# States' tokens in rounds of 64 + 32 + 32 rows, a new order of the small steps, and another order of the first loads

## The chip, the core and the metric

The kernel runs on one core of one Trainium2 chip. The metric is the device time of one execution in microseconds (us). Every run of the kernel before is listed with its median; one more execution was profiled, and all times of single instructions come from that one.

## The reference, cut to what matters

`x` has 8 batches of 8 heads x 512 tokens x 64, `state` 8 batches of 8 heads x 32 x 64. Attention goes both ways, and its two results are joined along the token axis, so a batch has 512 tokens read from the states (below: text tokens) and 32 read from the text (below: states' tokens). A switch layer with 8 experts follows; all is float32.

```python
xread = softmax(x @ state.T * 0.125) @ state        # 512 rows a batch
sread = softmax(state @ x.T * 0.125) @ x            #  32 rows a batch
t = concat([xread, sread])  ->  4352 rows of 512    # heads side by side
e = argmax(t @ w_gate); g = softmax(t @ w_gate)[e]
out = g * (relu(t @ w1[e]) @ w2[e])                 # w1: 512 x 1024, w2: 1024 x 512
```

On the given inputs all 512 text tokens of a batch choose one expert: 1, 2, 7, 0, 0, 0, 3 and 4 for batches 0 to 7. The states' tokens are handled in two halves of 128 rows (batches 0 to 3 and 4 to 7). Counted with the reference, the experts 0 to 7 get 0, 56, 0, 29, 1, 40, 0 and 2 rows of the first half, and 32, 64, 0, 0, 0, 0, 0 and 32 of the second.

## The kernel before, in words

Every engine runs its instructions in the order in which the program writes them; waits are semaphores. TensorE is PE in the profile, VectorE DVE, ScalarE ACT, GpSimd POOL, SyncE SP. A float32 product of 128 x 512 is two PE instructions, so counts of matmuls in the profile are twice those of the calls.

**Start** (L118 to L169, L715 to L736). SP loads the states of batch 0, `x` of batch 0, the other states and `x` of batch 1. Then it reads the guessed expert of batch 0 (`guess`, L201) and loads that expert's w1 (2 MB, `load_w1`, L237) and w2 (2 MB, `load_w2`, L421). Pool meanwhile clears DRAM: 12 DMAs for the two `g_dram` buffers (L162) and 6 for the two `ss_dram` buffers (L166).

**Batch 0** (`in_full`, L427) is computed in full: `G = state @ w1` (`states_w1`, L399), 8 products `ph` with a relu, and 4 x 8 products `py`.

**Batches 1 to 7** (`batch`, L546) use that a relu over a batch's tokens is often all on or all off. `lists(b)` (L458) makes G, transposes it (`pgt`), sorts the hidden units with a count (`rank`, L497) and scatters their rows into `g_dram` by 8 indirect DMAs from Pool (L509). `fetch(b)` (L515) loads the sorted rows back (`gp`, 3 DMAs) and gathers rows of w2 by 6 indirect DMAs from Pool (`gather`, L524, tile `w2c`). `mask(b)` (L534) zeroes unused rows on DVE. `batch(b)` then makes `pgu` (4 transposes), `pm` (2 x 4 products with `w2c`), `phu` (2 x 2 products) and `py`.

**Attention** of a batch is `front` (L285: transposes and softmax on DVE and ACT, products `pa`) and `back` (L308: transposes of `a2`, products `pw`, `pl`, routing, `pq`, `pcnt`; it loads `x` two batches ahead).

**The states' tokens** (`sort_states`, L591; `rounds`, L641). A half's 128 rows are scattered into `ss_dram` by expert in groups of 32 rows, each group of one expert. A round takes 4 groups: it loads its 128 rows (`xg`), transposes them (`ptx`), and multiplies by w1 (tile `pgh`, two halves) and, after another transpose (`pth`), by w2 (tile `pgy`, two halves). Each half is 4 parts; a part is one slot of a ring of weights (`s`), of 4 tiles of 256 KB, one per group, loaded by SP under a condition that skips groups without rows. `four` (L665) runs a part's 4 products of 32 columns each. The ring has 4 slots, and `fetch(4)` refills it after each half. The first half of the states' tokens has 2 rounds, the second 1; more rounds run only if `more` is above 0 at the end.

**The order by hand.** `inserts` (L813) takes a string for each place between PE's large products; each letter there runs one step of a generator: A attention (`back(b)` and `front(b+1)` a step each), S `lists`, F `fetching`, M `masking`, R the states' tokens, K constants. Batches 1 to 7 share one string of 13 places (L831). Place 1 is behind `pgu`, 2 to 4 inside `pm`, 5 and 6 behind the two `phu`, 7 to 12 between the `py`; in it the scatters of the next batch (last step of `lists`) stand at place 3, the loads of `fetch` and the first three gathers at 6, the mask and the other gathers at 8.

Of the kernel before, what the change touches and what calls it, by code (L numbers as in the profile page):

```python
# [20 lines left out]
def kernel(  # L21
# [57 lines left out]
    NT = 2  # L79
    NG = 12  # L80
    NR = NG // 4
    MAIN = (2, 1)
    RING = 4

# [6 lines left out]
    st_dram = dram.tile([B * NS, DM], FP32)  # L91
    ss_dram = [dram.tile([NG * 32, XW], I32, name=f"ss_dram{t}") for t in range(NT)]
    g_dram = [dram.tile([CAPP + CAPU, GW], FP32, name=f"g_dram{i}") for i in range(2)]
# [29 lines left out]
    load_states(2, B - 1, B)  # L123
    load_x(1, sp)

# [19 lines left out]
    rev8 = iota("rev8", [128, E], [[-1, E]], base=E)  # L145
    jio = iota("jio", [128, NG], [[1, NG]])
    pos8 = iota("pos8", [128, NFC], [[128, NFC]], step=1)
# [10 lines left out]
    gp.memset(blank[:], 0)  # L158
    for i in range(2):
        for r in range(0, CAPP + CAPU, 128):  # L160
            n = min(128, CAPP + CAPU - r)
            gp.dma_start(out=g_dram[i][ds(r, n)].bitcast(I32), in_=blank[0:n, 0:GW])  # L162
    gp.memset(blank[:, DM + 1:DM + 2], FAR)
    for t in range(NT):
        for r in range(NR):
            gp.dma_start(out=ss_dram[t][ts(r, 128)], in_=blank[:])  # L166

# [243 lines left out]

    rings = [sst.tile([128, 4, 512], FP32, name=f"s{i}") for i in range(RING)]

# [7 lines left out]
    def load_w2(e):  # L421
        w2x = [ring() for _ in range(2)]
        for u in range(2):
            sp.dma_start(out=w2x[u][:], in_=moe_w2[ds(e, 1), ts(u, 512)].rearrange("o (c p) f -> p (o c) f", p=128))
        return w2x

    def in_full(G, a, w2x, store, insert=None):  # L427
        hx = [ring() for _ in range(2)]
        for f in range(NFC):
            ph = bank(name="ph")  # L430
            for g in range(2):
                pe.matmul(ph[:], lhsT=G[g][:, ts(f, 128)], rhs=tokens_of(a)[:, g], start=(g == 0), stop=(g == 1))
            relu(hx[f // 4][:, f % 4], ph[:])
            if insert:
                insert()
        for c in range(NC):
            py = bank(name="py")
            for f in range(NFC):
                pe.matmul(py[:], lhsT=hx[f // 4][:, f % 4, ts(c, 128)], rhs=w2x[f // 4][:, f % 4, :],
                          start=(f == 0), stop=(f == NFC - 1))  # L440
                if insert and f == 3:
                    insert()
            store(c, py)
            if insert:
                insert()
# [69 lines left out]
    def fetch(b):  # L515

        t = gps[b] = ffn.tile([128, NP + NU, GW], FP32, tag="gp", bufs=2, name="gp")
        gp.dma_start(out=t[:, 0:NP + 1], in_=g_dram[b % 2][0:CAPP + 128].rearrange("(j p) k -> p j k", p=128))
        for u in range(2):
            gp.dma_start(out=t[ts(u, 64), NP + 1], in_=g_dram[b % 2][ds(CAPP + 128, 64)])  # L520
        w2cs[b] = []
        gather(b, 3)

# [64 lines left out]

    eg = [const.tile([128, NR, 2, 4], I32, name=f"eg{t}") for t in range(NT)]

    def sort_states(t):  # L591
# [11 lines left out]
        for c in range(NDC):  # L603
# [8 lines left out]
        pe.matmul(pr[:, 1, :], lhsT=ones_b[:], rhs=oh[:, NX + t, :], start=True, stop=True, skip_group_check=True)  # L612
        small = lambda n, w=E, dt=FP32: att.tile([128, w], dt, tag=n, name=n)
        ng_i, ng, cum, base, rk = small("t_ni", dt=I32), small("t_ng"), small("t_cum"), small("t_base"), small("t_rk")
        dve.tensor_scalar(ng_i[:], pr[:, 1, :], 31.0, None, ALU.add)
        dve.tensor_scalar(ng_i[:], ng_i[:], 5, None, ALU.logical_shift_right)
        dve.tensor_copy(out=ng[:], in_=ng_i[:])
        dve.tensor_tensor_scan(cum[:], ng[:], none[:, 0:E], 0.0, ALU.add, ALU.add)
        dve.tensor_tensor(base[:], cum[:], ng[:], ALU.subtract)
        dve.scalar_tensor_tensor(rk[:], base[:], 32.0, pr[:, 0, :], ALU.mult, ALU.add)  # L620
        dve.tensor_tensor(rk[:], rk[:], oh[:, NX + t, :], ALU.mult)
        slot, slot_i = small("t_sl", 1), small("t_si", 1, I32)
        dve.tensor_reduce(slot[:], rk[:], AX.X, ALU.add)
        dve.tensor_copy(out=slot_i[:], in_=slot[:])
# [3 lines left out]
            out=ss_dram[t][:], out_offset=bass.IndirectOffsetOnAxis(ap=slot_i[:, 0:1], axis=0),  # L628
            in_=srow[:].bitcast(I32), in_offset=None, bounds_check=NG * 32 - 1, oob_is_err=False)
        ge = att.tile([128, NG, E], FP32, tag="t_ge", name="t_ge")  # L630
        dve.tensor_tensor(ge[:], jio[:].unsqueeze(2).to_broadcast([128, NG, E]),
                          cum[:].unsqueeze(1).to_broadcast([128, NG, E]), ALU.is_ge)
        eg_f = small("t_eg", NG)
        dve.tensor_reduce(eg_f[:], ge[:], AX.X, ALU.add)
        dve.tensor_scalar(eg_f[:], eg_f[:], float(E - 1), None, ALU.min)
        dve.tensor_copy(out=eg[t][:, :, 0], in_=eg_f[:].rearrange("p (r q) -> p r q", q=4))
        dve.tensor_scalar(eg[t][:, :, 1], jio[:].rearrange("p (r q) -> p r q", q=4), cum[:, E - 1:E], None, ALU.is_lt)
        dve.tensor_scalar(more[:, t:t + 1], cum[:, E - 1:E], -4.0 * MAIN[t], 0.0, ALU.add, ALU.max)
        yield

    def rounds(t, r0, r1):  # L641
# [9 lines left out]
        def fetch(n):  # L651
            for _ in range(n):
                if parts:
                    r, kind, k, half = parts.pop(0)
                    if r not in ex:
                        round_in(r)
                    w = ring()
                    for q in range(4):
                        src = (moe_w1[ds(ex[r][q], 1), ts(k, 128), ts(half, 512)] if kind == 1
                               else moe_w2[ds(ex[r][q], 1), ts(k, 128), :])  # L660
                        sp.dma_start(out=w[:, q], in_=src.rearrange("o p f -> p (o f)"),
                                     cond=ex[r][4 + q], bounds_check="skip_entire_dma")
                    have[r, kind, k, half] = w

        def four(dst, lhsT, r, kind, k, half, start, stop):  # L665
            w = have.pop((r, kind, k, half))
            for q in range(4):
                pe.matmul(dst[ts(q, 32), :], lhsT=lhsT[:, ts(q, 32)], rhs=w[:, q, :], start=start, stop=stop,
                          skip_group_check=True)

        round_in(r0)
        fetch(RING)
        for _ in range(2):
            yield
        for r in range(r0, r1):
# [46 lines left out]
    load_w1(0, expert_of(eb, 0))  # L722
    w2x = load_w2(expert_of(eb, 0))
    for t in std[1:]:
        act.copy(t[:, :, 64:128], t[:, :, 0:64])
        act.copy(t[:, :, 128:160], t[:, :, 0:32])
    next(f0)
    next(f0)
# [34 lines left out]

    attended, done, summed, listed, fetched = [0], [0], [0], [0], [0]

    def attention():
        for b in range(B):
            while done[0] < b - 3:
                yield
            for _ in run(back(b), *([front(b + 1)] if b + 1 < B else [])):  # L770
                yield
            attended[0] = b + 1
            yield

# [9 lines left out]
    def fetching():  # L784
        for b in range(1, B):
            while listed[0] < b or done[0] < b - 1:
                yield
            fetch(b)
            fetched[0] = b
            yield  # L790
            while summed[0] < b - 1:
                yield
            gather(b, NP + NU - 3)
            yield

    def masking():
        for b in range(1, B):
            while b not in w2cs or len(w2cs[b]) < NP + NU:
                for k in "SF":
                    next(todo[k], None)  # L800
# [9 lines left out]

    todo = {"A": attention(), "S": listing(), "F": fetching(), "M": masking(), "R": tokens(), "K": late_constants()}

    def inserts(plan):  # L813
        steps = iter(plan.split(","))

# [4 lines left out]

    next(todo["A"])
    G = [sst.tile([128, F], FP32, tag=n, name="G0") for n in ("sh", "shT")]
# [4 lines left out]
    load_next_w1(1)  # L827
    in_full(G, aTs[0], w2x, store_batch(0), inserts("A,A,AK,AAS,AAS,AS,AAS,AS,AAS,SAA,SAA,FAA,FSAA,SAA,SA,SAM"))
    for b in range(1, B):
        done[0] = b  # L830
        batch(b, inserts("FS,SA,SR,SA,SR,FS,SA,MSR,A,R,A,AR,R"))  # L831
    for k in "ASFMR":
        for _ in todo[k]:
            pass
# [27 lines left out]

    with tc.If(number(rest_i[0:1, 0:1], B * E + NT * NG) > 0):
        with tc.If(number(n_i[0:1, 1:2], NT * NG) > 0):
            for t in range(NT):
# [102 lines left out]
```

## Time and profile before

| what | us |
|---|---|
| median of 9 runs (lowest, highest) | 469.44 (464.05, 476.36) |
| the profiled execution | 467.46 |
| its span, first to last instruction | 465.6 |
| PE busy | 395.1 (85%) |
| DVE busy | 197.9 (42%) |
| ACT busy | 123.8 (27%) |
| Pool busy | 133.2 (29%) |
| mean granted clock of TensorE | 0.949 of full speed |
| moved by DMA | 105.54 MB, 46.9% of the engines' time on SP's queue, 16.7% on Pool's |
| first `pgu` of batches 1 to 7 | 117.2, 156.0, 220.7, 287.9, 327.8, 377.6, 436.0 |
| last product's end | 459.6 |

Busy times are those of each engine alone and lie beside one another. A matmul's end is modelled, so PE's busy time holds some waiting; where PE is seen to wait, the releaser in brackets behind a row tells for what. A chain row "DMA s" means that the step after it could not start before that transfer of the states' weights had landed.

### The profile page before, as it was taken

To read this page: it belongs to the slowest core of one execution; us is meant where nothing else is said; L and a number is where in the kernel's file an instruction comes from. 1 tells how busy PE (TensorE), PEld (TensorE's weight loads), DVE (VectorE), ACT (ScalarE), POOL (GpSimd) and SP (SyncE) were. 2 spreads that over 40 slices of the span, in tenths; PEclk is the share of its full clock that TensorE was granted. 3 is DMA by queue.
4 is the path that set the end of the run, shared out by engine and by line. 5 is a ranking of instruction groups with operands and counts; after the bars stand their busy time and mean duration, and the time that the engine had idled before them with its cause. 6 is when DMAs were issued, how large, how long until landed. Compare 5 with 4: busy or idle time off the path is not lost.

```text
span 465.6 us, 9341 instructions
## 1 busy us (share of the span) xinstructions
PE 395.1 (85%) x3288; PEld 171.7 (37%) x3288; DVE 197.9 (42%) x586; ACT 123.8 (27%) x226; POOL 133.2 (29%) x166
## 2 busy tenths in 40 slices
PE   5639798897999997889898999899998068999994
PEld 3515355443544444214323424244343032242341
DVE  3915999985639753800432732234234020020200
ACT  2612534414333431301303222222332010120221
POOL 5400000355165152500253300544164206150000
PEclk9859999999898999989998999999999569999998
DMA  8996172248445598999998988749116968999302
GB/s 205 327 318 216 65 268 86 82 141 288 166 148 151 181 320 258 306 363 309 296 296 290 342 308 270 236 120 365 53 46 186 310 206 238 342 366 373 134 2 94
DMA packets 56517, 105.54 MB, mean 227 GB/s; under 512 B 9303, under 2 KB 18850, under 8 KB 56464
## 3 DMA queue, kind: packets, MB, share of 16 engines
q1 hardware_dynamic: 41936, 70.79, 46.9%
q0 software_dynamic: 9392, 25.68, 16.7%
q10 hardware_dynamic: 5136, 8.41, 4.9%
q8 instruction: 28, 0.46, 0.4%
q14 instruction: 25, 0.20, 0.2%
HBM read 95.99 MB, written 20.62 MB: 250 GB/s over the span
## 4 chain that ended last, share of the span: by engine, by line
PE 35%; DMA 15%; issue 5%; POOL 3%; DVE 2%; ACT 1%; SPq 0%; ACTq 0%; POOLq 0%
PE py L51 12%; DMA s<-in_moe_w_dram 10%; PE pm L51 5%; PE pgh L51 4%; PE pgy L51 4%; PE phu L51 4%; DMA xg<-ss_dram 2%; DMA g_dram<-gt,to 2%; POOL g_dram L51 1%; PE pG L51 1%; PE pgt L51 1%; POOL w2c L51 1%; PE pa L51 1%; ACT y L51 1%; PE pth L51 1%
## 5 line engine op out<-in xcount | busy, mean ns | idle before, releaser
L51 POOL DMA_INDIRECT g_dram<-gt,to x56 | 55.7, 994 | 190.0 <-ACT a L51 67.6
L51 PE MATMUL py<-M,aT 128*128 128x512 f32 x112 | 55.8, 621 | 1.1 <-DVE cnt L51 0.9
L51 POOL DMA_INDIRECT w2c<-in_moe_w_dram,gp x42 | 44.0, 1048 | 40.8 <-DMA gp<-g_dram 30.1
L51 PE MATMUL pm<-w2c,gp 128*128 128x512 f32 x112 | 53.6, 613 | 0.5 <-ACT y L51 0.5
L51 PE MATMUL pgh<-s,sxT 128*32 128x512 f32 x192 | 45.6, 610 | 8.0 <-DMA s<-in_moe_w_dram 7.1
L51 PE MATMUL py<-w2c,hu 128*128 128x512 f32 (+1 forms) x112 | 43.9, 617 | 0.0
L51 PE MATMUL pgy<-s,shT 128*32 128x512 f32 x192 | 39.0, 599 | 3.8 <-DMA s<-in_moe_w_dram 3.7
L51 DVE BATCH_NORM_STATS2 bn<-gt 128x6 f32<-128x256 f32 x56 | 20.5, 414 | 44.8 <-ACT gt L51 44.8
L51 ACT ACTIVATE y<-py,gw 128x512 f32<-128x512 f32 x32 | 22.0, 687 | 63.3 <-PE py L51 56.8
L51 PEld LDWEIGHTS py<-M,aT 128*128 128x128 f32 x112 | 20.3, 194 | 27.2 <-issue 25.5
L51 PE MATMUL py<-s,s 128*128 128x512 f32 x64 | 29.3, 603 | 0.0
L51 PE MATMUL phu<-aT,Gu 128*128 128x512 f32 x56 | 28.4, 638 | 0.1
L51 PEld LDWEIGHTS pm<-w2c,gp 128*128 128x128 f32 x112 | 20.2, 196 | 21.6 <-issue 20.9
L51 PE MATMUL pG<-w1t,stT 64*32 64x512 f32 x256 | 19.1, 664 | 8.3 <-DMA w1t<-in_moe_w_dram 8.3
L51 DVE COPY G<-pG 128x512 f32<-128x512 f32 x16 | 11.0, 688 | 33.2 <-PE pG L51 33.2
L51 DVE TENSOR_SCALAR gp<-gp,mk 128x256 f32<-128x256 f32 x42 | 12.3, 358 | 29.8 <-DMA gp<-g_dram 29.7
L51 PEld LDWEIGHTS pgh<-s,sxT 128*32 128x32 f32 x192 | 8.3, 109 | 42.6 <-DMA s<-in_moe_w_dram 33.3
L51 ACT COPY gt<-pgt 128x512 f32<-128x512 f32 x28 | 15.7, 589 | 25.7 <-PE pgt L51 14.4
L51 PEld LDWEIGHTS py<-w2c,hu 128*128 128x128 f32 (+1 forms) x112 | 15.0, 189 | 19.8 <-issue 19.4
L51 POOL DMA_DIRECT2D gp<-g_dram x21 | 14.3, 690 | 27.4 <-DMA g_dram<-gt,to 10.4
L51 PE MATMUL pa<-xt,stT 32*32 32x128 f32 x1024 | 18.1, 295 | 2.5 <-DVE xt L51 2.3
L51 PEld LDWEIGHTS pgy<-s,shT 128*32 128x32 f32 x192 | 8.3, 108 | 32.2 <-DMA s<-in_moe_w_dram 23.0
(182 smaller groups left out, 472.5 us busy)
## 6 DMA issues: line engine op xcount, KB each, us to landing
s<-in_moe_w_dram SPq DMA_DIRECT2D x192, 256.0 KB, 4.8
w1t<-in_moe_w_dram SPq DMA_DIRECT2D x8, 2048.0 KB
x_nat<-in_x_dram SPq DMA_DIRECT2D x16, 512.0 KB, 4.5
out_dram<-y ACTq DMA_DIRECT2D x32, 256.0 KB, 3.8
gp<-g_dram POOLq DMA_DIRECT2D x7, 642.5 KB, 6.4
s<-in_moe_w_dram SPq DMA_DIRECT2D x2, 1024.0 KB, 24.7
ss_dram<-blank POOLq DMA_DIRECT2D x6, 257.0 KB, 8.2
g_dram<-blank POOLq DMA_DIRECT2D x10, 128.5 KB, 9.8
```

What stands on the lines that cost most here:

```text
L51: ins = getattr(self.engine, name)(*args, **kw)
```

## The change

Three things are changed together.

1. The groups of the states' tokens. A round has one group of 64 rows and two of 32 (`COLS`) in place of four of 32. An expert's rows go into whole groups of 64; a remainder of over 32 takes another 64, a smaller one a group of 32. A part is then 3 tiles of 256 KB. The ring has 5 slots of 3 tiles in place of 4 of 4. `sort_states` computes the places with more small DVE instructions: 29 in place of 9 up to `slot_i`.
2. The order. Attention's one generator is split into `backs` (B) and `fronts` (T). `in_full` gets 24 places in place of 16. In batches 1 to 7 the scatters move from place 3 to 7, the loads of `fetch` and all 6 gathers to place 10, just behind the attention steps of places 7 to 9; the mask follows at once at 10. The steps R get a list for each batch (`pieces`). One step R of the second half, the last, is left over and runs behind batch 7.
3. The first loads. w1 of batch 0 goes ahead of `x` of batch 1 in SP's queue, w2 behind it. The clearing of `g_dram` and `ss_dram` (12 and 8 DMAs) moves from Pool to SP, behind w2.

The core of the diff:

```diff
-    NG = 12
-    NR = NG // 4
+    NR = 4
+    COLS = ((0, 64), (64, 32), (96, 32))
     MAIN = (2, 1)
-    RING = 4
+    RING = 5
...
-    load_x(1, sp)
...
-    for i in range(2):
-        for r in range(0, CAPP + CAPU, 128):
-            n = min(128, CAPP + CAPU - r)
-            gp.dma_start(out=g_dram[i][ds(r, n)].bitcast(I32), in_=blank[0:n, 0:GW])
...
+    def clear():
+        for i in range(2):
+            for r in range(0, CAPP + CAPU, 128):
+                n = min(128, CAPP + CAPU - r)
+                sp.dma_start(out=g_dram[i][ds(r, n)].bitcast(I32), in_=blank[0:n, 0:GW])
+        for t in range(NT):
+            for r in range(NR):
+                sp.dma_start(out=ss_dram[t][ts(r, 128)], in_=blank2[:])
...
-    rings = [sst.tile([128, 4, 512], FP32, name=f"s{i}") for i in range(RING)]
+    rings = [sst.tile([128, 3, 512], FP32, name=f"s{i}") for i in range(RING)]
...
-        gather(b, 3)
+        gather(b, NP + NU)
...
-                    for q in range(4):
+                    for q in range(3):
...
         def four(dst, lhsT, r, kind, k, half, start, stop):
             w = have.pop((r, kind, k, half))
-            for q in range(4):
-                pe.matmul(dst[ts(q, 32), :], lhsT=lhsT[:, ts(q, 32)], rhs=w[:, q, :], start=start, stop=stop,
+            for q, (c0, n) in enumerate(COLS):
+                pe.matmul(dst[ds(c0, n), :], lhsT=lhsT[:, ds(c0, n)], rhs=w[:, q, :], start=start, stop=stop,
                           skip_group_check=True)
...
-        for _ in range(2):
-            yield
+        yield
...
     load_w1(0, expert_of(eb, 0))
-    w2x = load_w2(expert_of(eb, 0))
+    e0 = expert_of(eb, 0)
...
+    load_x(1, sp)
+    w2x = load_w2(e0)
+    clear()
...
+    def backs():
         for b in range(B):
-            while done[0] < b - 3:
+            while done[0] < b - 3 or b not in soft:
                 yield
-            for _ in run(back(b), *([front(b + 1)] if b + 1 < B else [])):
+            for _ in back(b):
+                turned[0] = b
                 yield
             attended[0] = b + 1
-            yield
+
+    def fronts():
+        for b in range(1, B):
+            for i, _ in enumerate(front(b)):
+                yield
+                while i == 1 and turned[0] < b - 1:
+                    yield
...
-    in_full(G, aTs[0], w2x, store_batch(0), inserts("A,A,AK,AAS,AAS,AS,AAS,AS,AAS,SAA,SAA,FAA,FSAA,SAA,SA,SAM"))
+    in_full(G, aTs[0], w2x, store_batch(0), inserts(
+        "TT,B,TK,BBT,TS,BS,BS,TTS,BS,TS,B,S,TS,T,B,S,BS,TT,F,BS,MTS,BS,TS,S".split(",")))
+    rest = ["S", "T", "B", "", "F", "B", "SBT", "ST", "SB", "SSM", "T", "ST", "S"]
+    pieces = {1: (9, 10, 11, 12, 13), 2: (1, 6, 7, 12), 3: (3, 4, 8, 10, 13), 4: (4, 8, 9, 13),
+              5: (9, 10, 11, 12, 13), 6: (1, 5, 6, 11), 7: (2, 3, 8)}
     for b in range(1, B):
         done[0] = b
-        batch(b, inserts("FS,SA,SR,SA,SR,FS,SA,MSR,A,R,A,AR,R"))
-    for k in "ASFMR":
+        batch(b, inserts([k + "R" * pieces[b].count(i + 1) for i, k in enumerate(rest)]))
+    for k in "BTSFMR":
```

With the steps counted through, the pieces of products with the states' weights (a piece is one half of `pgh` or `pgy`, 4 parts) stand in the batches 2, 3, 3, 3, 4, 4, 4, 5 (first half) and 6, 7, 7 and behind 7 (second half); before they stood in 2, 2, 2, 3, 3, 3, 3, 4 and four times in 6. With the counts above, the groups that have rows are 4 and 3 in the first half's two rounds and 4 in the second's round before, 3, 2 and 3 after; neither version has rows left for further rounds. Of attention, the strings of batch 0 held `front` of batches 1 to 4 and `back` of 0 to 3; they now hold `front` of 1 to 3 but for the last step, and `back` of 0 to 2.

## The prediction

> **What bounds the kernel now.** I read the two busy strips first, for the stages.
>
> ```profile
> PE   5639798897999997889898999899998068999994
> ...
> DMA  8996172248445598999998988749116968999302
> ...
> q1 hardware_dynamic: 41936, 70.79, 46.9%
> ```
>
> PE is idle at the start (slice 3 is 3) and again in slices 32 and 33 (0 and 6). The DMA engines are full exactly where the states' weights stream (slices 15 to 25, 34 to 37), so PE's nines there need a second look. The windows between the first `pgu` of each batch give it: after the span of time come PE, PEld, DVE, ACT, POOL busy, the granted clock, the DMA share and GB/s.
>
> ```profile
> 117.20:156.00 38.80, 37.90 (x346) 19.13 (x346) 24.58 (x79) 13.08 (x24) 16.58 (x17) 0.91 0.51 161
> 156.00:220.70 64.70, 57.45 (x443) 21.39 (x441) 27.44 (x84) 17.35 (x30) 17.57 (x19) 0.97 0.90 292
> 220.70:287.90 67.20, 62.44 (x473) 23.05 (x472) 25.31 (x68) 15.81 (x28) 18.27 (x19) 0.97 0.91 302
> 287.90:327.80 39.90, 38.70 (x239) 15.91 (x237) 14.51 (x53) 9.79 (x17) 16.98 (x18) 1.00 0.68 230
> 327.80:377.60 49.80, 30.76 (x131) 14.23 (x130) 12.84 (x60) 10.90 (x19) 17.67 (x19) 0.85 0.54 174
> 377.60:436.00 58.40, 55.02 (x204) 18.02 (x202) 7.39 (x30) 7.06 (x12) 15.96 (x17) 0.98 0.85 287
> 436.00:459.60 23.60, 23.54 (x62) 9.92 (x60) 1.57 (x11) 5.73 (x10) 1.02 (x1) 1.00 0.16 59
> ```
>
> Batch 7 has its own products alone: 23.6 us. Batches 2, 3 and 6, with the states' rounds, take 58 to 67 and sit at a DMA share of 0.85 to 0.91; batch 5 loses time to something else. The chain of waits names both, and clean prices:
>
> ```profile
> 191.88 8.21 DMA s<-in_moe_w_dram
> 200.22 7.25 DMA s<-in_moe_w_dram
> ...
> 260.13 3.57 PE pgh L51 x32
> 263.70 2.77 PE py L51 x6
> ...
> 317.71 2.58 PE py L51 x6
> ...
> 370.84 5.71 DMA xg<-ss_dram
> ```
>
> A piece with the states' weights (4 parts) costs 3.57 us when its weights are there. The twelve pieces in fact took 95 us by PE's timeline (191.3 to 209.2 for the worst), so some 52 us go to waiting for weights. Before `xg`, PE stood 17.7 us in batch 5: the scatter into `ss_dram` sat behind six gathers in Pool's queue. A float32 product is 2.58/3 = 0.86 us; the 2.77 behind `pgh` says that a change of tile shape costs 0.1 to 0.2.
>
> Last, Pool's timeline, for the chain that feeds the next batch, and PE's first product with w1:
>
> ```profile
> 228.96 1.01 POOL L51 DMA_INDIRECT g_dram<-gt,to  x1 [33.35 <-DVE to L51]
> ...
> 244.88 2.01 POOL L51 DMA_DIRECT2D gp<-g_dram  x3 [4.06 <-DMA g_dram<-gt,to]
> 253.17 1.06 POOL L51 DMA_INDIRECT w2c<-in_moe_w_dram,gp  x1 [6.28 <-DMA gp<-g_dram]
> ```
>
> ```profile
> 30.32 3.67 PE L51 MATMUL pG<-w1t,stT 64*32 64x512 f32 x32 [8.34 <-DMA w1t<-in_moe_w_dram]
> ```
>
> From `rank` on PE (84.9, 124.1, 162.5, 225.9, 293.2, 333.4, 383.1) to the first gather (109.4, 143.8, 188.0, 253.2, 313.6, 354.4, 409.9) are 24.5, 19.7, 25.5, 27.3, 20.4, 21.0 and 26.8 us; with 7.0 to land (median of the 42 gathers) the chain from `rank` to the first `pm` is 27 to 28 where the DMAs are free and 32 to 34 where states' weights stream (31 in batch 0, where DVE is 95% busy).
>
> **The start.** By the GB/s strip some 8.4 MB had moved when w1 was in at 30.3: states and `x` 0 (1.5 MB), `x` 1, w1, the clearing (3) and part of w2. After, w1 has only the 1.5 MB ahead. Issued at about 9 as before, 2 MB at the 320 GB/s of slices 2 and 3 are in by 17. Next late is attention of batch 0 on PE, whose transposes end at 22.0. G starts at 22: -8.3. The clearing (3.5 MB, 20 DMAs) now stands in SP's queue ahead of w1 of batch 1 and `x` 2: 10.1 MB in all go first, 1.5 by 9 and the rest at 320 GB/s by 36, so that w1 is in at about 43, against a need at about 40: +3, bounds 0 and +10.
>
> **Batch 0.** By the timeline's rows PE has from G to `rank` of batch 1: G 2.2, guess 2.0, eight `ph` 15.6, G of batch 1 2.2, `pgt` 2.4, 1.25 `py` 4.6, two `pa` 3.8, `pw`, `pl`, `pq`, `pcnt` and transposes of two batches 6: 39. DVE has 33 there (two attention fronts instead of 3.5). With the 3 of waiting, `rank` is at 64 (before 84.9), and with a chain of 30 to 31 batch 1 starts at 95 (before 117.2). This is the largest gain and comes with a debt: one batch of attention more in the later batches.
>
> **Batches 1 to 7.** `rank` of the next batch moves from place 3 to 7, so a batch is the work ahead of place 7 plus the longer of the chain and the work behind it. Ahead: `pgu` and `pm` 7.3, `phu` 3.5 (rows of batch 7), attention 2.3, together 13.1. Behind: `py` 12.8, `pq` and `pcnt` 0.5, `pa` 1.75, G 2.04, `pgt` 1.75: 18.9. That is shorter than any chain, so pieces behind place 7 are free until 28 to 34 are full.
>
> **The price of a piece** is the disputed one. One part is now a 64-column product and two of 32 columns. If all three run side by side as four of 32 do, it is 3.57. If the 64 runs alone and the two 32s after it, a part is 2 x 0.86 and two changes of shape at 0.15: 2.03, a piece 8.1. Below 3.57 nothing speaks for it: the streamed 512 columns stay. What overlaps in this trace has one shape (32 instructions 128*32 in 3.57; 16 of 64*32 in 1.02); no two shapes overlap, and the change of shape is where time is lost. That row is the nearest to the new mix: I take 8.1 and keep 3.57 as the other end.
>
> The Trainium skill speaks against this edit: "TensorEngine Tiling (Array Packing)", Key Properties, says that changing the tiling mode, not only the tile, drains the array, and 128*64 and 128*32 are two modes in its list. By it the sum is the 444 below, by the rows of equal shape 413; no row of this trace has two column shapes in one part.
>
> The weights: 11 groups of 4 MB become 8, so 12 MB (some 40 us at 300 GB/s) leave. Pieces now stand 6 to 20 us apart and a refill is 3 MB or less (9 us), so I cost the rest of the waiting at nothing. Its cover is the pieces' own spacing; where it is gone (first round, 12 MB in 57 us beside 6 MB of other traffic, 324 GB/s, as much as saturated windows show) it would cost up to 5.
>
> `sort_states` has 20 more DVE instructions ahead of its scatter, 0.19 each: 3.8. From `prs` to landed `xg` were 13.7 us (154.9 to 168.6, the landing 5.2), now 17.5. First half: 13.2 of PE work lies between, 4.3 of stall behind `rank`, inside the chain. Second half: 10.3 between, 7.2 of stall ahead of `rank`, on the path. Against that the 17.7 of batch 5 goes, since the scatter now stands ahead of Pool's others.
>
> The sum of stages: 95 to batch 1; batch 1 13.1 + 28 = 41.1; batch 2 13.1 + 31.9 (work 27.6 and the stall) = 45.0; batch 3, with one piece and `pth` ahead, 22.1 + 35.7 (18.9, two pieces, `ptx`) = 57.8; batch 4 21.2 + 36.0 = 57.2; batch 5 13.1 + 28 = 41.1; batch 6 18.8 + 30 = 48.8; batch 7 23.6, two pieces, `pth` = 40.7. Behind it the last piece 8.1, DVE 0.75, scatter 1.0, landing 3.7: 13.5, where before the stores took 6.0. Together 440.2. The profiled execution was 1.9 above its span, and the median is 2.0 above that execution: **444**.
>
> **Rivals.** (a) The shapes run side by side: pieces 3.57, every batch but 7 bound by the chain. Batch 2 44.1, batch 3 17.6 + 34, batch 4 16.7 + 30, batch 7 31.7, tail 9: 409.1, median **413**, chance 0.30.
> (b) Slower: the Pool chain, moved behind `phu`, becomes the bound of every batch. Work ahead of place 7 sums to 101.4 over batches 1 to 6, so with 95, 40.7 and 13.5 the old span is met at a chain of 35.8 us in all six. For it: three chains of before were 32.5 to 34.3, and Pool now has the `ss_dram` scatter and `xg` ahead of two of them. Against: those three fell in saturated stretches, and 12 MB leave. At 39 us it is 484.6, median **488**; chance 0.11.
> (c) The gains of the start and of batch 0 hold, but refills (5), the first w1 of the queue (7 more) and chains at 31 in the free batches cost most of the rest: 440.2 + 18 = 458, median **462**; chance 0.08.
> (d) The rows do not fit and further rounds run: five, of 16 parts at 0.89 at least, +71: about 515. The counts (2 and 3 groups, 1 and 2) fill the second half's round exactly, so there is no reserve, but a round of four groups, also full, sufficed before: 0.01.
>
> **How the numbers follow.** 444 has 0.50; its own range is 430 to 462 (chains 27 to 33, w1 0 to +10). The range reaches down over most of (a) and up to (c): 405 to 466. Of no change a measurement of this kernel can tell about 1%, 4.7 us: faster 0.83, the same 0.06, slower 0.11.
>
> **What would show it.** `pG` at 22 instead of 30; batch 1's `pgu` near 95; `pgh` x24 (a clean piece has 24 instructions now) at 8.1 or at 3.6; waits for `s` almost gone; q1 12 MB lighter but for the clearing; `w2c` waits on PE at each batch's start; 7 us before the second half's `ptx`. A clean piece of 3.6 would make the number too high by 31; chains over 36 would make it wrong in sign.

## The result, and the profile after

The median of ten runs after the change is 486.68 us (482.96 to 490.06), beside 471.70 us (31 runs) of the kernel before on the same chip: a ratio of 1.0386, 95% interval 1.0346 to 1.0425. The change makes the kernel slower by 3.9%; the forecast was 444. The profiled execution of after took 486.32 us, its span 484.5, at a mean granted clock of 0.929 (before 0.949). A run that took over 1.5% more than the fastest of its kernel is kept in the medians below and left out of the ratios and intervals.

The busy strips and SP's queue on the page of after:

```profile
PE   5695999936993899999999999999997769599992
...
DMA  6999431852244369597589653794116485974620
...
q1 hardware_dynamic: 37792, 61.76, 39.4%
```

SP's queue moves 9 MB less, and the DMA strip has 8 nines where before had 14. PE's strip is all nines from slice 15 to 30, through those stretches in which the DMAs have become freer: PE did not get idle there, it got busier. Its low slices are 9, 10 and 13 around batch 1 (3, 6 and 3), where before had 9, 7 and 9, and 31, 32, 33 and 35 around batches 6 and 7.

The windows of after, cut at the first `pgu` of batches 1 to 7, at the end of the last `py` and at the end (columns as before: stretch, PE, PEld, DVE, ACT, POOL busy, clock, DMA share, GB/s):

```profile
0.00:109.53 109.53, 85.13 (x1187) 45.38 (x1187) 66.05 (x165) 35.81 (x70) 18.78 (x38) 0.92 0.67 213
109.53:159.76 50.23, 38.67 (x344) 19.93 (x345) 28.51 (x77) 16.73 (x32) 17.01 (x18) 0.84 0.36 110
159.76:208.79 49.03, 45.30 (x363) 19.37 (x364) 33.12 (x117) 13.95 (x26) 17.58 (x19) 0.93 0.63 212
208.79:269.94 61.15, 58.92 (x419) 21.32 (x418) 26.64 (x69) 15.13 (x27) 18.93 (x19) 1.00 0.85 291
269.94:329.98 60.04, 58.52 (x415) 20.80 (x413) 23.27 (x67) 17.21 (x30) 16.80 (x17) 1.00 0.64 212
329.98:371.00 41.02, 39.97 (x242) 17.20 (x241) 13.77 (x51) 10.52 (x19) 13.11 (x15) 1.00 0.25 79
371.00:421.24 50.24, 36.37 (x94) 13.18 (x94) 10.65 (x70) 8.20 (x14) 15.42 (x17) 0.88 0.71 230
421.24:467.50 46.26, 43.84 (x116) 14.10 (x116) 3.10 (x7) 5.41 (x9) 6.11 (x6) 0.91 0.54 174
467.50:484.50 17.00, 8.04 (x26) 1.34 (x24) 2.52 (x13) 1.37 (x2) 1.02 (x1) 0.79 0.13 50
```

Batches 2 and 3 fell from 64.7 and 67.2 us to 49.0 and 61.2, batch 5 from 49.8 to 41.0 and batch 6 from 58.4 to 50.2. Batch 1 rose from 38.8 to 50.2, batch 4 from 39.9 to 60.0, batch 7 from 23.6 to 46.3, and the stretch behind the last `py` from 6.0 to 17.0. Batch 0 ends 7.7 us earlier, where the forecast had 22.

The rows of PE's timeline that answer to the steps of the forecast, ahead of and around batch 1:

```profile
21.65 2.84 PE L51 MATMUL pG<-w1t,stT 64*32 64x512 f32 x32
...
46.91 1.96 PE L51 MATMUL pG<-w1t,stT 64*32 64x512 f32 x16 [5.31 <-DMA w1t<-in_moe_w_dram]
...
109.53 1.11 PE L51 MATMUL pgu<-ident,gp 128*128 128x128 f32 x4 [7.85 <-DVE cnt L51]
113.96 6.24 PE L51 MATMUL pm<-w2c,gp 128*128 128x512 f32 x8 [3.31 <-ACT gt L51]
```

G starts at 21.65, 8.7 earlier, as forecast. Then three waits follow: w1 of batch 1 is late (5.3, where the forecast had 3), `pgu` waits for DVE (7.9) and `pm` for ACT (3.3). For the last two the forecast had no term of their own beside the chain. SP's timeline shows why w1 is late (the second column is the time over which SP issued the group):

```profile
16.83 12.82 SPq L51 DMA_DIRECT2D g_dram<-blank  x12
29.75 5.38 SPq L51 DMA_DIRECT2D ss_dram<-blank  x8
37.23 0.39 SPq L51 DMA_DIRECT2D w1t<-in_moe_w_dram  x1
```

The 20 clearings take SP 18.2 us to issue; w1 of batch 1 is issued at 37.2, behind them (at 28.7 in e11 below, where it goes ahead of them). Pool's timeline has the chain to the first gather, and DVE's the instruction that waits with it:

```profile
92.78 2.08 POOL L51 DMA_DIRECT2D gp<-g_dram  x3 [6.07 <-DMA g_dram<-gt,to]
102.96 1.15 POOL L51 DMA_INDIRECT w2c<-in_moe_w_dram,gp  x1 [8.11 <-DMA gp<-g_dram]
...
109.79 0.99 POOL L51 DMA_INDIRECT w2c<-in_moe_w_dram,gp  x1 [0.30 <-issue]
```

```profile
102.79 1.95 DVE L51 TENSOR_SCALAR gp<-gp,mk 128x256 f32<-128x256 f32 x6 [10.97 <-DMA gp<-g_dram]
```

The mask stands at place 10 right behind the loads of `gp`, so DVE stands still for 11 us, and attention's softmax, `cnt` and with them `pgu` are queued behind it. PE is left with 0.1 us of work from 101.6 to 109.5, and pays for that twice, as windows around `pm` show (the clock is third from the right):

```profile
109.53:113.90 4.37, 1.11 (x4) 0.71 (x4) 2.31 (x7) 2.09 (x7) 0.99 (x1) 0.50 0.49 151
113.96:117.00 3.04, 3.04 (x4) 1.49 (x5) 2.11 (x9) 1.60 (x3) 0.00 (x0) 0.50 0.22 86
120.90:124.50 3.60, 3.60 (x11) 1.69 (x10) 1.41 (x3) 1.33 (x3) 0.00 (x0) 1.00 0.02 5
```

After the waits the granted clock is 0.50 until past 117: the first eight instructions of `pm` take 6.24 us, the next eight 3.60. The Trainium skill ("TensorE: Matmul & The Clock Gate", Part 1) describes this: an idle array is put back to half its clock and gets the full one only after some microseconds of work.

Last, a piece with the states' weights, from PE's timeline, and the weight loads of the last piece:

```profile
199.30 8.01 PE L51 MATMUL pgh<-s,sxT 128*64 128x512 f32 x24 [0.46 <-ACT gt L51]
```

```profile
467.53 0.19 PEld L51 LDWEIGHTS pgy<-s,shT 128*64 128x64 f32 x2 [0.76 <-issue]
...
468.54 0.14 PEld L51 LDWEIGHTS pgy<-s,shT 128*32 128x32 f32 x4 [0.81 <-issue]
...
469.52 0.19 PEld L51 LDWEIGHTS pgy<-s,shT 128*64 128x64 f32 x2 [0.84 <-issue]
```

A part takes 2.0 us: 1.0 for the group of 64 columns, then 1.0 for the two groups of 32. Twelve pieces at 8.0 are 96 us; with their waits for weights they took 95 before. The 9 MB less bought nothing in the pieces: PE now computes where it had waited.

### The profile page after: what moved, and what is told of

It is laid out like the page before. It is cut to its first block, busy times and chain, and to the rows that moved or that the text cites. A ratio compares the mean times of both kernels' runs of the same rounds, so it can differ in the third digit from the quotient of the medians.

```text
span 484.5 us, 8934 instructions
## 1 busy us (share of the span) xinstructions
PE 414.7 (86%) x3192; PEld 172.6 (36%) x3192; DVE 207.6 (43%) x634; ACT 124.3 (26%) x226; POOL 124.8 (26%) x149
## 4 chain that ended last, share of the span: by engine, by line
PE 44%; DMA 8%; DVE 3%; ACT 3%; issue 2%; POOL 1%; ACTq 1%; POOLq 0%; SPq 0%
PE py L51 11%; PE pgh L51 10%; PE pgy L51 8%; PE pm L51 6%; PE phu L51 4%; DMA s<-in_moe_w_dram 2%; DMA gp<-g_dram 2%; ACT y L51 2%; DMA out_dram<-y 1%; PE pa L51 1%; DMA xg<-ss_dram 1%; DMA g_dram<-gt,to 1%; DMA w2c<-in_moe_w_dram,gp 1%; PE pG L51 1%; PE pw L51 1%
## 5 line engine op out<-in xcount | busy, mean ns | idle before, releaser
L51 POOL DMA_INDIRECT g_dram<-gt,to x56 | 57.1, 1020 | 203.4 <-DVE r L51 83.6
L51 PE MATMUL pm<-w2c,gp 128*128 128x512 f32 x112 | 59.7, 678 | 6.8 <-ACT gt L51 3.3
L51 PE MATMUL py<-M,aT 128*128 128x512 f32 x112 | 53.8, 602 | 0.0
L51 PE MATMUL pgh<-s,sxT 128*64 128x512 f32 (+1 forms) x144 | 48.5, 613 | 0.5 <-ACT gt L51 0.5
L51 PE MATMUL pgy<-s,shT 128*64 128x512 f32 (+1 forms) x144 | 48.1, 609 | 0.0
L51 PEld LDWEIGHTS pm<-w2c,gp 128*128 128x128 f32 x112 | 22.7, 216 | 34.3 <-issue 26.9
L51 DVE TENSOR_SCALAR gp<-gp,mk 128x256 f32<-128x256 f32 x42 | 13.3, 376 | 38.6 <-DMA gp<-g_dram 38.3
L51 PEld LDWEIGHTS py<-M,aT 128*128 128x128 f32 x112 | 20.0, 190 | 24.8 <-issue 22.6
L51 PE MATMUL phu<-aT,Gu 128*128 128x512 f32 x56 | 28.1, 630 | 0.0
L51 PE MATMUL pgt<-ident,G 128*128 128x128 f32 x112 | 18.3, 287 | 8.8 <-ACT gt L51 7.5
L51 PE MATMUL py<-s,s 128*128 128x512 f32 x48 | 22.5, 599 | 0.0
L51 POOL DMA_DIRECT2D gp<-g_dram x21 | 14.4, 698 | 30.9 <-DMA g_dram<-gt,to 10.1
L51 PEld LDWEIGHTS pgh<-s,sxT 128*64 128x64 f32 (+1 forms) x144 | 8.1, 118 | 39.6 <-issue 31.5
L51 PEld LDWEIGHTS pgy<-s,shT 128*64 128x64 f32 (+1 forms) x144 | 8.0, 117 | 37.2 <-issue 31.4
```

Source lines behind the costliest of these rows:

```text
L51: ins = getattr(self.engine, name)(*args, **kw)
```

## Experiments

Every set of runs shared one chip and its own runs of the kernel before: e1 to e4 are set one, e5 to e8 two, e9 to e12 three, e13 to e16 four, e17 and e18 five. Sets one, two and three each had a chip of their own, four and five the same one. The kernel before took 504.9, 472.7, 467.3, 501.0 and 500.0 us in sets one to five, so times are compared within a set, and ratios to before across sets. The last section comes back to that difference.

### Is it the mixed shapes?

**e1_same_shape** and, in the second set, **e6_same_shape_again**: the changed kernel, with four products of 32 columns a part; the first two read the same weight tile, so transfers stay as changed.

```diff
-            for q, (c0, n) in enumerate(COLS):
-                pe.matmul(dst[ds(c0, n), :], lhsT=lhsT[:, ds(c0, n)], rhs=w[:, q, :], start=start, stop=stop,
+            for c, q in enumerate((0, 0, 1, 2)):
+                pe.matmul(dst[ts(c, 32), :], lhsT=lhsT[:, ts(c, 32)], rhs=w[:, q, :], start=start, stop=stop,
```

> The changed kernel with the same groups, loads, order and first loads; only the group of 64 rows is multiplied as two products of 32 columns that read the same weight tile, so that all four products of a part have one shape. Theory A (products of two column shapes do not overlap, and that is what the rounds cost): a piece takes 3.6 us instead of 8.0; by the stages of the prediction, 31 us leave the span, so about 453 us span and 456 us median. Theory B (the new order is what costs, through waits on Pool's chain, VectorE and PSUM banks): the pieces shrink, but the chain fills the room; less than 12 us leave, so 474 us or more.

466.96 us, ratio 0.9205 (0.9155 to 0.9255), with 3.64 us a piece. The changed kernel itself was not in this set, so the difference was taken again:

**e5_after_again**, the changed kernel, beside e6.

> The changed kernel itself, unaltered, so that it stands beside the next three on one chip. Both theories: 1.03 to 1.05 of the kernel before on this chip, as measured first (1.039).

> e1_same_shape again, beside the changed kernel on one chip. Theory A (two column shapes in one part do not overlap): 25 to 35 us under e5_after_again. Theory B (the order's waits): less than 12 us under it.

e5 took 485.43 us (ratio 1.0265, 1.0231 to 1.0299), e6 457.32 (0.968 of before by the medians). The four runs of e6 lie between 451.65 and 462.31, too far apart for an interval: it is 28.1 us under e5 by the medians, 31.7 by the mean of its two fastest runs. The clean piece in e6, from PE's timeline:

```profile
198.29 3.64 PE L51 MATMUL pgh<-s,sxT 128*32 128x512 f32 x32 [1.75 <-ACT gt L51]
```

More instructions (32 for 24) over the same weights take less than half the time, because the four column groups have one shape.

**e2_two_of_64** asks whether it is the width of 64 or the mix: two products of 64 columns a part. It leaves out the third expert's weights, and the rows of columns 96 to 127 are multiplied by the second expert's.

```diff
-            for q, (c0, n) in enumerate(COLS):
+            for q, (c0, n) in enumerate(((0, 64), (64, 64))):
```

> The changed kernel with two products of 64 columns a part in place of 64 + 32 + 32; the third expert's weights are loaded but not used, so rows of the third group come out with the second group's weights. Theory A: two products of one shape overlap, a part takes 0.9 us and a piece 3.6. If instead a 64-column product is slow by itself (each one 0.86, one after the other), a part takes 1.8 and a piece 7.2. The span follows e1_same_shape within 3 us in the first case.

One execution took 476.86 us. Its span, 475.1, was expected within 3 us of e1's and is 6.6 above it, which one execution cannot explain. Its PE timeline has the piece:

```profile
214.16 3.65 PE L51 MATMUL pgh<-s,sxT 128*64 128x512 f32 x16
```

Two groups of 64 run side by side as well as four of 32. It is the mix that runs one after the other. The rule of the Trainium skill weighed in the forecast ("TensorEngine Tiling (Array Packing)", Key Properties: a change of the tiling mode drains the array) agrees with these three prices, 8.01, 3.64 and 3.65. The drain itself is in no trace here.

### Which part of the change is worth what

**e3_old_order**: new rounds (mixed shapes) and new first loads, with the old order. **e4_start_only**: the new first loads alone.

e3 against the changed kernel (with the generators of before), and e4 against the kernel before:

```diff
-        batch(b, inserts([k + "R" * pieces[b].count(i + 1) for i, k in enumerate(rest)]))
+        batch(b, inserts("FS,SA,SR,SA,SR,FS,SA,MSR,A,R,A,AR,R"))
```

```diff
-    load_x(1, sp)
...
-    w2x = load_w2(expert_of(eb, 0))
+    e0 = expert_of(eb, 0)
...
+    load_x(1, sp)
+    w2x = load_w2(e0)
+    clear()
```

> The new rounds (64 + 32 + 32, mixed shapes) and the new first loads, but the order of before: its strings, its attention steps, its gathers in two threes. Theory A alone (order harmless): pieces 8.0 each, twelve of them 96 us as the 95 us of before, first loads -8: about 458 us span; the changed kernel's 484 is then left unexplained by 26. Theory B (order costs): the same 458, and this is the point: 20 us or more below the changed kernel. If the order were a gain, this kernel would be slower than 484.

> The kernel before with the new first loads alone (w1 first in the queue, clearing on SyncE's queue behind w2). By the prediction: pG at 22 instead of 30, w1 of batch 1 late by 3 to 6 us; a gain of 3 to 8 us, 464 to 469 us against 471.7. Rival: attention in batch 0 is bound by VectorE (95% busy there), so that the earlier start is waited away again and batch 1 starts near 117 as before: no change within 2 us.

e3: 518.73 us, ratio 1.0243 (1.0162 to 1.0324), pieces 8.01. e4: 502.37, ratio 0.9958 (0.9912 to 1.0005). The first loads alone are worth little, and the rounds with mixed shapes cost under the old order too: e3 is 16.4 us above e4. For e3 both theories had 458 us of span, 20 or more below the changed kernel; its ratio lies beside the 1.0265 of the changed kernel in set two instead. The changed kernel was not run on this chip, so what the order costs there with mixed shapes is not measured.

**e7_start_rounds_32**: first loads and rounds as in e6, but the old order. **e8_rounds_32_only**: the rounds as in e6, first loads and order of before.

> The new first loads and the new rounds with products of one shape, in the order of before. Against e6_same_shape_again it differs by the order alone. Theory A: the order spreads the pieces and hides the weights, so e6 is faster by 5 to 20 us. Theory B: the order's waits (VectorE behind the mask, gt in one buffer) cost 10 us or more, so e7 is faster than e6 by that.

> The kernel before with the new rounds alone, as products of one shape. 12 MB fewer weights; before, the pieces wait some 52 us for weights by the trace. Theory A: a gain of 20 to 40 us over the kernel before. If the wait only moves (to the Pool chain of the next batch), the gain is under 10 us.

e7: 435.48, ratio 0.9224 (0.9178 to 0.9270). e8: 442.19, ratio 0.9335 (0.9256 to 0.9414). All four of the set shared a chip, so the change can be taken apart there by the medians: from 472.65, the rounds with one shape -30.5, the first loads -6.7, the new order +21.8, the mixed shapes +28.1, together 485.4. With the runs that the ratios use, and the two fastest of e6, it is -32.5, -4.6, +18.3 and +31.7. The first loads are not clear of noise (the intervals of e7 and e8 overlap), and the order's price was taken with equal shapes only. Without the new order and the mix, the change would have made the kernel 7.8% faster there.

Where the order's 18 to 22 us lie is seen in the windows of e6, and then of e7 (batch 0; batches 1 to 4; batch 5 to the end):

```profile
0.00:108.59 108.59, 82.91 (x1185) 44.75 (x1187) 66.15 (x165) 35.90 (x70) 18.79 (x38) 0.94 0.67 215
108.59:310.08 201.49, 175.84 (x1586) 80.70 (x1591) 107.55 (x320) 63.25 (x114) 65.33 (x68) 0.92 0.66 217
310.08:454.10 144.02, 110.61 (x515) 44.40 (x512) 32.50 (x150) 25.53 (x43) 41.47 (x44) 0.88 0.55 183
```

```profile
0.00:115.29 115.29, 92.04 (x1402) 51.16 (x1405) 84.83 (x204) 43.00 (x85) 19.41 (x39) 0.93 0.66 205
115.29:306.59 191.30, 178.96 (x1491) 77.57 (x1495) 95.83 (x307) 55.88 (x99) 69.02 (x74) 0.95 0.72 240
306.59:431.80 125.21, 101.08 (x392) 40.90 (x390) 25.21 (x124) 25.11 (x42) 35.43 (x38) 0.94 0.56 191
```

The new order gains 6.7 in batch 0, loses 10.2 in batches 1 to 4 and 18.8 from batch 5 on. PE's work is the same in sum (369.4 and 372.1), but it has moved: 9.1 us less ahead of batch 1 (one batch of attention), 9.5 more behind batch 4 (the second half's round, which needs all of attention). The rest is idle PE: stretch less busy time is 25.7, 25.7 and 33.4 in the three stretches of e6, 23.3, 12.3 and 24.1 in e7, 25 us more.

### Two waits of the new order, taken one by one

**e9_mask_late**: e6 with the mask moved to the end of a batch, so that DVE does not stand behind the loads of `gp`.

```diff
-        "TT,B,TK,BBT,TS,BS,BS,TTS,BS,TS,B,S,TS,T,B,S,BS,TT,F,BS,MTS,BS,TS,S".split(",")))
-    rest = ["S", "T", "B", "", "F", "B", "SBT", "ST", "SB", "SSM", "T", "ST", "S"]
+        "TT,B,TK,BBT,TS,BS,BS,TTS,BS,TS,B,S,TS,T,B,S,BS,TT,F,BS,TS,BS,TS,SM".split(",")))
+    rest = ["S", "T", "B", "", "F", "B", "SBT", "ST", "SB", "SSBTSF", "T", "ST", "S"]
...
-        batch(b, inserts([k + "R" * pieces[b].count(i + 1) for i, k in enumerate(rest)]))
+        batch(b, inserts([k + "R" * pieces[b].count(i + 1) + "M" * (i == 12) for i, k in enumerate(rest)]))
```

> e6_same_shape with the mask alone moved: from place 10 (right behind the gathers) to 13, and in batch 0 from place 21 to 24. Theory C: the mask waits in VectorE's queue for gp to land, and attention's softmax, queued behind it, holds ScalarE and through the PSUM banks TensorE; then some 20 us of TensorE's waits (pgu on VectorE's cnt 7.2, pgt on ScalarE's gt 6.3, pm on gt 3.3 and others) go and the time falls by 5 to 12 us against e6 (0.968 of the kernel before on the chip of e6, 0.921 on that of e1). Rival: gt has one buffer and waits for the scatters, or the chain of Pool ends later anyway: less than 3 us.

455.15 us, ratio 0.9713 (0.9642 to 0.9784); e6 had 0.968. No gain, but the run does not tell what DVE's wait is worth, since it puts another in its place. In batch 2 `gp` has landed at 144.8, when the first gather starts; the mask now stands behind other work of DVE and runs 9.5 us later, and `pgu` can only start once it runs, at 154.7. `pgu` stands 5.3, 4.1, 6.3 and 5.1 us in batches 1 to 4. So the price of the wait stays open.

**e10_pieces_early**: e6 with all four pieces of the second half in batch 6.

```diff
-              5: (9, 10, 11, 12, 13), 6: (1, 5, 6, 11), 7: (2, 3, 8)}
+              5: (9, 10, 11, 12, 13), 6: (1, 5, 6, 8, 10, 11, 12, 13), 7: ()}
```

> e6_same_shape with the second half's four pieces all in batch 6 (places 8, 10, 12, 13) in place of 11 and three behind. Theory D: the new order costs because attention ends one batch later, so the second half's rounds come too late to fill batch 6's wait for Pool's chain, and lengthen batch 7 and the tail; then 10 to 16 us go against e6. Rival: the chain from the scatters at place 7 is the price, batch 6 is full already: only the tail is won, about 6 us or less.

458.08 us, ratio 0.9801 (0.9753 to 0.9849). Batch 7 fell to 23.6 us and the tail to 6.3, but batch 6 grew from 49.4 to 70.4: its round starts at place 5, and the pieces then wait for weights. Moving pieces alone only moves the 20 us.

### A version that is faster than both

**e11_clear_later**: e7 with the clearing issued behind w1 of batch 1. **e12_best**: the same, and in batch 5 the second half's steps some places earlier.

```diff
     w2x = load_w2(e0)
-    clear()
...
         yield
+        clear()
         dve.tensor_scalar(U128[:], colf[:], iota_p[:, 0:1], None, ALU.is_gt)
```

```diff
-        batch(b, inserts("FS,SA,SR,SA,SR,FS,SA,MSR,A,R,A,AR,R"))
+        batch(b, inserts("FSR,SAR,RS,SA,SR,FS,SA,MSR,A,,A,AR,R" if b == 5 else
+                         "FS,SA,SR,SA,SR,FS,SA,MSR,A,R,A,AR,R"))
```

> e7_start_rounds_32 with the 20 clearing transfers put behind w1 of batch 1 and x of batch 2 in SyncE's queue. TensorE's wait of 5.7 us for that w1 goes. If the first stage is bound by TensorE, 4 to 6 us are won against e7 (0.922 of the kernel before); if VectorE binds it, 0 to 2.

> e11_clear_later with the second half's sorting drawn forward in batch 5, so that its scatter into ss_dram stands ahead of the next scatters and gathers in Pool's queue. The wait of 14.7 us for xg before ptx goes: 8 to 14 us under e11, about 0.885 to 0.90 of the kernel before. Rival: the chain for batch 6, one scatter later, takes the place: under 4 us.

e11: 426.84 us, ratio 0.9148 (0.9096 to 0.9201), beside e7's 0.9224 (its interval overlaps e11's); w1 of batch 1 is issued at 28.7 (e7 38.1), PE no longer waits for it (e7 5.7), and the first `pgu` of batch 1 came at 107.95 where e7 had 115.29. e12: 422.32 us, ratio 0.9027 (0.8975 to 0.9079), 4.5 under e11 where 8 to 14 were expected. The wait for `xg` (15.7 in e11) is gone, but PE now waits 9.4 for ACT ahead of a `py` in batch 5.

### The order once more, by halves

**e13_chain_early** puts `rank`, scatters, `fetch` and mask of e6 back to places 3, 6 and 8. **e14_attention_early** lets batch 0 carry as much of attention as before and puts the pieces at the places of before. **e15_both_early** does both. **e16_same_shape_again** is e6, their reference.

In e13 and e15:

```diff
-    rest = ["S", "T", "B", "", "F", "B", "SBT", "ST", "SB", "SSM", "T", "ST", "S"]
+    rest = ["S", "T", "SB", "S", "S", "FB", "SBT", "MST", "SB", "BT", "T", "ST", "S"]
```

In e14 and e15:

```diff
-        "TT,B,TK,BBT,TS,BS,BS,TTS,BS,TS,B,S,TS,T,B,S,BS,TT,F,BS,MTS,BS,TS,S".split(",")))
+        "TT,B,TK,BBT,TS,BS,BS,TTS,BS,TS,B,S,TS,T,B,S,BS,TT,F,BS,MTS,BTS,TBTS,BTBTBTS".split(",")))
...
-    pieces = {1: (9, 10, 11, 12, 13), 2: (1, 6, 7, 12), 3: (3, 4, 8, 10, 13), 4: (4, 8, 9, 13),
-              5: (9, 10, 11, 12, 13), 6: (1, 5, 6, 11), 7: (2, 3, 8)}
+    pieces = {1: (3, 5, 8, 10, 12, 13), 2: (5, 8, 10, 12, 13), 3: (3, 5, 8, 10, 12, 13), 4: (3, 12, 13),
+              5: (3, 5, 8, 10, 13), 6: (3, 5, 8, 10, 12), 7: ()}
```

> The kernel of e6 with one edit in the order: rank, the scatters into g_dram and the fetch of the next batch go back from places 7 and 10 to places 3, 6 and 8, as before; attention, the states' pieces and batch 0 stay as changed. Theory E (the 22 us that the new order costs lie in the place of the chain: rank at place 7 leaves it 19 us of work where it needs 30): 15 to 22 us under e14's partner e16, batches 6 and 7 from 99.9 us to the end towards 80. Theory F (they lie in attention and the pieces coming a batch later): within 5 us of e16. Theory G (each alone moves the wait to the other): within 8 us of e16, and only e15 falls by 20.

> The kernel of e6 with the other half of the order undone: batch 0 carries as much of attention as before (to the scores of batch 4), and the states' pieces stand at the places of before (second half's round from batch 6, place 3, done in batch 6); rank and the scatters stay at place 7, the fetch at 10. Theory E: within 5 us of e16. Theory F: 15 to 22 us under e16. Theory G: within 8 us of e16.

> e13 and e14 together: chain, attention and pieces at the places of before, in the split generators of the changed kernel. All theories: 18 to 26 us under e16, about as e7 (435.5 on the second chip), since what is left of the new order (gathers in one call, ptx one call earlier, batch 0's string) is small. Higher than e16 minus 15 would mean that batch 0's string costs the rest.

> The kernel of e6 beside the other three, as their reference on this chip: 0.96 to 0.98 of the kernel before if the chip is like the second and third, 0.92 if it is like the first.

| run | us | ratio | 95% interval |
|---|---|---|---|
| e13_chain_early | 491.82 | 0.9861 | 0.9754 to 0.9968 |
| e14_attention_early | 496.62 | 0.9944 | 0.9907 to 0.9981 |
| e15_both_early | 481.88 | 0.9624 | 0.9512 to 0.9736 |
| e16_same_shape_again | 470.92 | 0.9447 | 0.9350 to 0.9545 |

All three theories fell on this chip: no way back helped, and e15, which all three had at 18 to 26 us under e16, was 11 above it. Before took 501 here, 473 in the set with e6 and e7. So the last two runs asked whether the sign belongs to the chip: **e17_old_order_again** is e7, **e18_both_early_again** is e15. They came to the chip of set four again.

> The kernel of e7 (changed first loads, rounds as products of 32 columns, the old order) beside e18. Theory H (what an order costs depends on the chip: where PE has issue gaps between attention's small products, the new order hides them in the chain's waits, elsewhere it only moves work late): on a chip where the kernel before takes about 500 us, a ratio above e16's 0.945; where it takes about 470, the 0.92 of e7. Theory G (the old order is better by some 20 us on any chip): 0.90 to 0.925 on either.

> The kernel of e15 (new generators, but chain, attention and pieces at the places of before). If chain, attention and pieces are the whole difference of the orders: within 1% of e17 on either chip. If batch 0's string holds part of it: over 2% above e17.

e17: 484.16 us, ratio 0.9712 (0.9648 to 0.9777). e18: 480.05, ratio 0.9581 (0.9482 to 0.9681). e17 is above e16's ratio with its whole interval, while in set two the same kernel e7 was 18 to 22 us faster than e6. On the chip of sets four and five, where before takes 500 us, the new order is the faster one by some 13 us; on that of set two, where before takes 473, the slower one by 18 to 22. Each sign is that of one chip. e18 is 0.8% under e17, so chain, attention and pieces are nearly all that the two orders differ in there. The halves were not run where before takes 470, so which of them holds the price there stays open.

The windows of e17 beside those of e7 above show where the chip matters (same program, same cuts):

```profile
0.00:117.80 117.80, 90.32 (x1404) 49.77 (x1405) 85.06 (x204) 42.90 (x85) 19.57 (x39) 0.94 0.64 205
117.80:353.52 235.72, 202.17 (x1494) 86.53 (x1495) 95.05 (x307) 56.01 (x99) 68.21 (x73) 0.88 0.60 196
353.52:480.50 126.98, 104.65 (x392) 41.99 (x390) 25.41 (x124) 24.90 (x42) 34.68 (x37) 0.93 0.54 182
```

Of the 48.7 us between e17 and e7, 44.4 lie in batches 1 to 4, which hold attention's small products. About half is idle PE (21.2 more), half slower work: PE's busy time is 23.2 higher, at a granted clock of 0.88 for 0.95. For e16 beside e6 the same stretch grew by 17.9 only (219.44 against 201.49). The list of PE's waits of e17 shows what is new (total us, times, longest):

```profile
PE pw L51 <- issue: 15.2, 23, 1.2
...
PE pa L51 <- issue: 8.1, 16, 1.1
PE pl L51 <- issue: 7.5, 12, 1.0
```

These 30.8 us, 27.8 of them in batches 1 to 4, wait for nothing that the profile shows. In e7 none of the three has such a wait; in e16 they come to 13.4 (10.1, 1.9 and 1.4). The other traces divide in the same way: in all ten of sets one, four and five the three come to between 12.7 and 30.8 us, in the eight of sets two and three and in those of before and after to 0.2 at most. With these gaps the new order has fewer of them (13.0 in e1, 13.4 in e16) than the old one (23.1 in e3, 30.8 in e17). That it hides them where PE would wait for the chain anyway fits, but no run shows it.

## Why the prediction was wrong

The mechanism that it thought disputed, it had right: a piece is 8.01 us (8.1 forecast), the waits for `s` are gone, q1 is 9 MB lighter (12 less the clearing), the second half's `ptx` waits 6.6 (7.2), G starts at 21.65 (22). The price of the piece was worked out from 0.86 a product and 0.15 a change of shape, so it is no luck. With the pieces of equal shape the forecast's own rival (a) had a span of 409.1; e6 is that case and has 454.1. It misses by 45.0, the main forecast by 44.3 (440.2 against 484.5). So the miss is in the stages, whatever a piece costs. Split at `rank`, as the forecast did (us, forecast then measured):

| stage | ahead of `rank` | from `rank` to the next `pgu` |
|---|---|---|
| batch 0 | 64 / 72.9 | 31 / 36.6 |
| batch 1 | 13.1 / 19.9 | 28 / 30.3 |
| batch 2 | 13.1 / 18.0 | 31.9 / 31.0 |
| batch 3 | 22.1 / 23.7 | 35.7 / 37.4 |
| batch 4 | 21.2 / 22.2 | 36.0 / 37.9 |
| batch 5 | 13.1 / 13.3 | 28 / 27.7 |
| batch 6 | 18.8 / 24.8 | 30 / 25.4 |

- **"`rank` is at 64 ... batch 1 starts at 95"** failed: +14.5. PE was at `rank` at 72.9: the wait for w1 was 5.3 where 3 was taken (inside the bounds; the clearing was priced by its bytes, and it was its 18.2 us of issue that held w1 back), and PE's rows took 44.5 us where 39 were counted (`ph` 18.1 for 15.6, at a clock of 0.88). Behind `rank`, the first gather came after 30.0 us (24.5 before), 10.2 of it the loads of `gp`; then DVE had mask, softmax and `cnt` to do before `pgu`.
- **The work ahead of place 7, "together 13.1"**, failed in batches 1, 2 and 6: +6.8, +4.9 and +6.0. I priced it by rows at the full clock, with nothing in the way. Batches 1 and 2 begin after an idle PE (7.9 and 7.5 us): the first eight instructions of `pm` take 6.2 and 5.7 us at the half clock (3.6 at the full one). And all three hold waits of their own: `pm` 3.3 for ACT in batch 1, `prs` 1.9 and 2.9 for DVE in batches 2 and 6. In batch 6 the sixteen of `pm` behind that wait take 8.8 (7.2) at a granted clock of 0.80, and the four `phu` behind the wait for `xg`, which was priced, 3.3 (1.9) at 0.56. Batches 3, 4 and 5, where PE came without a pause, are right within 1.6. PE's rows in batches 2 and 6:

```profile
162.78 0.19 PE L51 MATMUL prs<-oh,U 128*128 128x8 bf16 x1 [1.92 <-DVE oh L51]
162.88 5.66 PE L51 MATMUL pm<-w2c,gp 128*128 128x512 f32 x8
...
374.54 0.18 PE L51 MATMUL prs<-oh,U 128*128 128x8 bf16 x1 [2.91 <-DVE oh L51]
374.64 8.80 PE L51 MATMUL pm<-w2c,gp 128*128 128x512 f32 x16
...
391.78 1.09 PE L51 MATMUL ptx<-ident,xg 128*128 128x128 f32 x4 [6.62 <-DMA xg<-ss_dram]
392.66 3.34 PE L51 MATMUL phu<-aT,Gu 128*128 128x512 f32 x4
```

- **"the longer of the chain and the work behind it"** held: over batches 1 to 6 the second column is off by 0.1 in sum, from 2.3 over to 4.6 under, so that the sum is closer than the terms. Rival (b), a chain of 35.8 or more in all six batches, is not how it became slower; that its 488 lies beside the 486.68 is chance.
- **Batch 7 and the tail**: 46.3 for 40.7, 17.0 for 13.5. In batch 7 `pm` waits 1.9 for `w2c`, and its first four instructions take 3.8 at the half clock (1.9). This is the only wait for `w2c` on PE, where the forecast expected one at each batch's start. In the tail the piece is right, but the last counts on DVE are queued behind `ys` and end at 478.3; the step counted only the store. The chain that ended last ends with these counts; what fills the 6.2 us from there to the end of the span is in none of its rows, so this cause is not shown.
- **"This is the largest gain and comes with a debt"**: the debt was never priced against the old order. The forecast built the new order from rows and took the old span as it was; e6 against e7 shows the order at +18 to +22 on the chip of set two, where the forecast had it, with the first loads, as the only source of its 25 us.

By the medians of set two the mixed shapes leave -2.4 of the -30.5 that the rounds were worth; on the chip of set one they even made the rounds cost 16.4 (e3 against e4). On the chip of set two the new order then costs more than the first loads bring.

## What to carry to other kernels

Cut columns of the systolic array into groups of one width: in this kernel's float32 products 64 + 32 + 32 cost 8.01 us where 4 x 32 and 2 x 64 cost 3.64 and 3.65, and an expert of 64 rows can be two groups of 32 that read one weight tile. When an order of steps is moved, price the stretches behind an idle PE at half the clock (here behind 7.5 and 7.9 us of idle time, 2 to 2.6 us each), and what is pushed to the end of the program against the old order, stage by stage. Try an order on more than one chip before it is kept or dropped: the same two orders ended some 20 us apart in one direction and 13 in the other.

## What the runs showed of the hardware that was not expected

The same program took a span of 431.8 us in e7 and 480.5 in e17. From PE's timelines of batch 1, the 64 products `pw` of one batch, first in e7 and then in e17:

```profile
124.69 1.14 PE L51 MATMUL pw<-x_nat,a2T 128*32 128x64 f32 x64
```

```profile
126.67 1.15 PE L51 MATMUL pw<-x_nat,a2T 128*32 128x64 f32 x50
128.22 0.34 PE L51 MATMUL pw<-x_nat,a2T 128*32 128x64 f32 x6 [0.41 <-issue]
128.97 0.32 PE L51 MATMUL pw<-x_nat,a2T 128*32 128x64 f32 x4 [0.41 <-issue]
129.69 0.34 PE L51 MATMUL pw<-x_nat,a2T 128*32 128x64 f32 x4 [0.40 <-issue]
```

After 50 products at full pace, PE goes on in groups of 4 to 6, one every 0.72 to 0.75 us. One product's mean time is unchanged (229 ns against 233). What PE lacks in the gaps is not in the profile, and no run here tells whether it belongs to a chip or to its condition at that time: the two sets on one chip, taken one after the other, agree, and no chip was seen in both kinds. That stays open.
